# Moving four 1 MB zero fills within the order in which one Trainium2 core issues its stores

## The chip, the cores and the metric

The kernel runs on one core of a Trainium2 chip. The metric is the device time of one execution in microseconds (us); less is better. The core has a matrix engine (TensorE, PE in the profile), a vector engine (VectorE, DVE), a scalar engine (ScalarE, ACT), a general engine (GpSimd, POOL) and a synchronising engine (SyncE, SP). Data moves between device memory and on-chip memory by DMA. GpSimd and SyncE each issue DMAs on a queue of their own, and sixteen transfer engines carry out both queues.

## What is computed

The reference is one layer for a single token, forward and backward: the output and ten gradients.

```python
x = A_x
mod = (_silu(c) @ w_mod).reshape(c.shape[0], 6, 1, -1)
sa, ca, ga, sb, cb, gb = (mod[:, i].copy() for i in range(6))
h = _layernorm(x) * (1 + ca) + sa
x = x + ga * attention(h, k_cache, v_cache, wq, wo)   # last 4096 of 65536 positions
h = _layernorm(x) * (1 + cb) + sb
# FFN: D = 1024, F = 3584
g = jnp.einsum('bsd,df->bsf', h, w_gate)
u = jnp.einsum('bsd,df->bsf', h, w_up)
x = x + gb * jnp.einsum('bsf,fd->bsd', _sigmoid(g) * u, w_down)
...
_out, _vjp = jax.vjp(_f, A_x, A_k_cache, A_v_cache, A_wq, A_wo, B_w_gate, B_w_up, B_w_down, c, w_mod)
return (_out, *_vjp(grad_out))
```

Attention looks at the last 4096 of 65536 cached positions only. The gradients of the two caches have the full size, 64 MiB each, and are zero in the other 61440 positions. Writing those zeros is about half of all the bytes that the kernel moves.

## The kernel before

The zero region is cut into 120 pieces of 1 MB. The function `zero(n)` (line 153) takes the next n pieces from one list and issues each as one DMA from a tile of zeros, on GpSimd's queue (line 169). So a fill is not tied to any place in the program: the constants `Z_...` at the head of the file say how many fills stand at each point of GpSimd's instruction order, and the regions are taken in one fixed sequence. Every twelfth or thirteenth piece or so (`NARROW`) is written differently: a cursor reset, a small DMA and a DMA over 60 partitions that leaves out one of the transfer engines (lines 160 to 167).

GpSimd issues in program order. If an instruction waits, everything behind it on GpSimd waits too. Each of its DMAs uses one of eight semaphores in turn, and waits for the DMA eight places earlier to land. A fill after a matmul of the phase before the FFN also waits for that matmul ("pace").

The work is staged as follows: attention forward; the products for its weight gradients (`bch`, 64 chunks, paced by `Z_B`); folding of the modulation weights (`fold_half`, `fold_run`); then the FFN forward and backward in seven blocks of 512 hidden columns; then the remaining gradients of attention and of the modulation.

Before the FFN, `load_ug(0, ...)` issues four loads of w_up and w_gate for block 0. After them come the last chunks of `bch` with three fills (chunks 56, 58 and 60), the rest of the folding, `zero(Z_FOLD[0])`, the four loads of block 1, and `zero(Z_FOLD[1])`. `load_wd` loads the two halves of w_down on SyncE's queue.

Block 0 then runs: `front` (gate and up products), `gates` and `hh_ops` (sigmoid), `ffn_mm` (down product), `wd_ttr` (VectorE products with w_down), `wd_outer` (the gradient of w_down written over w_down by VectorE, and `store_wd` on GpSimd). This happens for two halves, and `zero(Z_FOLD[2])` follows. These are "the first w_down stores".

The loop over q then does, for each block:

- eight `ttr` on VectorE and eight `outer_act` on ScalarE, which overwrite the w_up and w_gate tiles of block q with their gradients; after the fourth, `store_ug(q, 0, 4)` and `zero(z[0])`, after the eighth, `store_ug(q, 4, 4)` and `zero(z[1])`;
- `front`, `gates`, `hh_ops` of block q + 1;
- first half of w_down of block q + 1, `load_ug(q + 2, 0, 4)`, its `store_wd`, then `zero(z[2])`;
- second half, its `store_wd`, `load_ug(q + 2, 4, 4)`, then `zero(z[3])`, and `load_wd(q + 2, ...)` on SyncE, which waits until the w_down stores have landed, since there is one w_down tile.

For the last block there is no next one, and `zero(z[2] + z[3])` follows its second `store_ug`. Here z is `Z_FFN[q]`.

Of the kernel before, what the change touches and what calls it, by code (L numbers as in the profile page):

```python
# [40 lines left out]
def spread(total, n):  # L41
    return [(i + 1) * total // n - i * total // n for i in range(n)]
# [8 lines left out]
Z_KC = [0] * 8  # L51
Z_SM = 4
Z_N = spread(31, 128)
Z_B = [n + (i in (31, 38)) for i, n in enumerate(spread(29, 43))] + [1, 1, 1, 1, 0] + [1, 1, 0, 1, 1, 0, 1, 1] + [1, 0, 1, 0, 1, 0, 0, 0]
Z_FOLD = (1, 1, 3)
Z_FFN = [(1, 1, 0, 1)] * 5 + [(1, 1, 1, 2), (1, 2, 1, 0)]
Z_END = (1, 2, 1, 0, 0)
@with_exitstack
def kernel(
# [93 lines left out]
    def zero(n, after=None):  # L153
        for _ in range(n):
            if len(zleft) <= keep[0]:
                return
            region, narrow_ = zleft.pop(0)
            first = None
            if narrow_:
                nc.gpsimd.inc_swdge_sem([], [], mode="reset_dge_cursor")  # L160
                n = nlen - ncount.pop()
                first = nc.gpsimd.dma_start(
                    out=rest[0:NS, 0:nlen * 128].rearrange("p (t x) -> p t x", t=2)[:, :, n * 64:(n + 1) * 64],
                    in_=zeros[0:NS, 0:64].rearrange("p (t x) -> p t x", t=1).broadcast_to([NS, 2, 64]))
                ins = nc.gpsimd.dma_start(
                    out=region[8:P, :].bitcast(FP32).rearrange("(t p) x -> p t x", t=2),
                    in_=zeros[0:60, :].rearrange("p (t x) -> p t x", t=1).broadcast_to([60, 2, ZW // 2]))
            else:
                ins = nc.gpsimd.dma_start(out=region.bitcast(FP32), in_=zeros[:, :])  # L169
            if after is not None:  # L170
                dep(first or ins, after)
# [437 lines left out]
    def mod_gb(ts_):  # L609
        ps = new_acc("g_ps")  # L610
        mod_tiles(ps, g_t, ts_, True, ts_[-1])
        if ts_[0] == 6:
            cp(gb, ps[:, 0:KD])
        else:
            addv(gb, gb, ps[:, 0:KD])
# [5 lines left out]
    def recent(mm, lag):  # L621
        last_mm.append(mm)
        return last_mm[-lag] if len(last_mm) >= lag else last_mm[0]
# [57 lines left out]
    def bch(n=1):  # L681
        for _ in range(n):
# [5 lines left out]
            for a in range(4):  # L688
                h = 4 * u + a
                for k in range(2):  # L690
                    mm = nc.tensor.matmul(bbank[p][k][:, :], lhsT=a4[:, p, h, :], rhs=wo_t[u][:, a, k * 512:(k + 1) * 512],  # L691
                                          start=(i == 0 and a == 0), stop=(i == 7 and a == 3))
            zero(Z_B[nbq - 1 - len(bq)], recent(mm, 3))
            if i == 7:
# [87 lines left out]
    def park(p, pl, tag):  # L782
        BT_ps[p] = pl.tile([P, D], BF16, name="BT_ps", tag=tag)
        for i in range(KD):
            nc.tensor.transpose(BT_ps[p][:, i * P:(i + 1) * P], B_t[p][:, i * P:(i + 1) * P], ident_bf[:, :])
# [64 lines left out]
    def load_wd(q, s):  # L850
        nc.sync.dma_start(out=wd_v[:, 2 * s:2 * s + 2, :], in_=wd_dram(B_w_down, q, s))
# [10 lines left out]
    def load_ug(q, j0, n):  # L862
        for k, view in ((0, wu_view), (1, wg_view)):
            nc.gpsimd.dma_start(out=ug_tile(q, k, j0, n), in_=ug_part(view, q, j0, n))
# [5 lines left out]
    def fold_half(t, k):  # L870
        ps = new_ps("fold_ps")
        for i in range(4):
            nb = 4 * k + i
            for x, src in enumerate((ga_t[t], cb_t[t], sb_t[t])):
                nc.tensor.matmul(ps[:, i * P:(i + 1) * P], lhsT=src[:, nb * P:(nb + 1) * P], rhs=ident_bf[:, :],  # L875
                                 start=(i == 0 and x == 0), stop=(x == 2), skip_group_check=True)
        nc.scalar.copy(out=w2_t[t][:, k * 512:(k + 1) * 512], in_=ps[:, :])  # L877
# [45 lines left out]
    fold_half(7, 1)  # L923
    zero(Z_FOLD[0])
    park(4, ppq, "pq")
    load_ug(1, 0, 4)
    load_ug(1, 4, 4)
    zero(Z_FOLD[1])
    mod_gb((0, 1, 2, 3, 4, 5))
# [48 lines left out]
    def wd_outer(q, s):  # L978
        for i in (2 * s, 2 * s + 1):
            outer_dve(wd_v[:, i, :], small[q % 2]["hh"][:, i:i + 1], b1k)  # L980
        store_wd(q, s)
# [30 lines left out]
    wd_outer(0, 1)  # L1012
    zero(Z_FOLD[2])
    load_wd(1, 0)
    load_wd(1, 1)
    for q in range(NB):
        z = Z_FFN[q]
        more = q + 1 < NB
# [315 lines left out]
```

## Time and profile before

| | |
|---|---|
| median of 6 runs | 600.74 us (600.02 to 601.30) |
| profiled execution | 600.27 us |
| span from its first to its last instruction | 598.5 us |
| PE / DVE / ACT / POOL busy | 68% / 55% / 48% / 28% of the span |
| moved by DMA | 246.64 MB, mean 412 GB/s |
| fills of 1 MB on GpSimd's queue | 111, median 14.6 us from issue to landing |
| gradient stores of the FFN (L868) | 28 of 512 KB, GpSimd waits 39.8 us for ScalarE before 8 of them |

Times in the profile count from the start of the span. A row of the timeline names the start, the duration, the engine, the line of the kernel, the operation, what it writes and reads, and, in brackets, how long the engine had been idle before and what ended that. A line can be that of a helper: line 169 is every full fill, line 854 every store of the gradient of w_down, line 864 every load of w_up or w_gate, line 868 every store of their gradients, line 851 every load of w_down after the first section. The share of the DMA engines can be above 1, since packets of one engine overlap.

### The profile page before, as it was taken

The page shows a single profiled execution, that of the slowest core. Times are in us where ns is not written, and L with a number is a line of the kernel's source. Part 1 is how long each engine was busy: PE and PEld are TensorE (multiplying, and loading weights), DVE is VectorE, ACT ScalarE, POOL GpSimd, SP SyncE. Part 2 cuts the span into 40 slices and gives each one's busy share as a digit, 9 for nine tenths or more (in the row PEclk, how much of TensorE's full clock was granted, in tenths as well). Part 3 has the DMA queues.
Part 4 walks back from the last instruction along what each step waited for, and adds up shares of the span by engine and source line. Part 5 has one row for each costly group of instructions (what it writes and reads, how often), then busy time and mean ns, then how long its engine had stood idle before and what let it go on. Part 6 is the DMA issues. An engine that isn't in the chain of part 4 may idle for free.

```text
span 598.5 us, 11048 instructions
## 1 busy us (share of the span) xinstructions
PE 408.3 (68%) x4587; PEld 273.7 (46%) x4612; DVE 326.9 (55%) x620; ACT 284.8 (48%) x429; POOL 166.5 (28%) x265
## 2 busy tenths in 40 slices
PE   3997688999999989999984435435444185776300
PEld 3995334334344545546664334434334155575200
DVE  3654499999511010160007495695686887878430
ACT  3489514567211014213225665865956864883200
POOL 0003123223222222222332244333343272122330
PEclk9999699999999999999995555555555586855555
DMA  8999999999999999999999999999999999999996
GB/s 349 419 418 422 412 426 417 426 424 426 428 420 427 422 426 425 425 422 423 422 402 408 418 405 409 409 411 410 410 411 416 413 408 414 421 423 426 426 415 253
DMA packets 45171, 246.64 MB, mean 412 GB/s; under 512 B 5253, under 2 KB 5253, under 8 KB 24712
## 3 DMA queue, kind: packets, MB, share of 16 engines
q0 software_dynamic: 38976, 216.55, 94.5%
q1 hardware_dynamic: 6096, 29.37, 12.5%
q8 instruction: 36, 0.59, 0.4%
q14 instruction: 15, 0.12, 0.1%
q10 hardware_dynamic: 48, 0.01, 0.0%
HBM read 60.30 MB, written 185.60 MB: 411 GB/s over the span
## 4 chain that ended last, share of the span: by engine, by line
PE 38%; DMA 32%; DVE 17%; ACT 5%; issue 5%; POOL 0%; ACTq 0%; POOLq 0%; SPq 0%; DVEq 0%
DMA out_dram<-arena 17%; PE b_ps L691 15%; PE n_ps L636 6%; DMA arena<-in_B_w_down_dram 6%; DMA out_dram<-zeros 5%; DVE arena L193 4%; DVE arena L206 3%; DVE arena L210 3%; DVE junk L210 3%; DMA arena<-in_B_w_gate_dram 3%; PE t_ps L598 2%; PE tp_wq L453 2%; PE w_ps L394 2%; PE tp_k L434 1%; ACT arena L241 1%
## 5 line engine op out<-in xcount | busy, mean ns | idle before, releaser
L169 POOL DMA_DIRECT2D out_dram<-zeros x111 | 60.8, 549 | 194.0 <-PE q_ps L471 50.7
L691 PE MATMUL b_ps<-arena 128*128 128x512 bf16 x494 | 113.4, 379 | 1.0 <-issue 0.2
L836 PE MATMUL tp_side<-ident_bf,arena 128*128 128x128 bf16 x432 | 51.7, 300 | 45.2 <-ACT arena L837 38.3
L837 ACT COPY arena<-tp_side 128x1024 bf16<-128x1024 bf16 x54 | 53.9, 1011 | 51.8 <-PE tp_side L836 51.5
L193 DVE TENSOR_TENSOR arena<-arena 128x2048 bf16<-128x2048 bf16 x64 | 76.5, 1224 | 2.3 <-PE n_ps L636 0.3
L691 PEld LDWEIGHTS <-arena 128*128 128x128 bf16 x512 | 48.7, 98 | 55.9 <-issue 2.9
L210 DVE CUSTOM_DVE_ANT_0 arena<-arena,scr 128x1024 bf16<-128x1024 bf16 x56 | 65.2, 1222 | 10.2 <-ACT scr L990 10.2
L636 PE MATMUL n_ps<-arena 128*128 128x512 bf16 x249 | 65.1, 378 | 6.9 <-DVE arena L193 5.0
L836 PEld LDWEIGHTS <-arena 128*128 128x128 bf16 x432 | 42.8, 139 | 49.6 <-issue 49.3
L241 ACT ACTIVATE arena<-scr,h 128x1024 bf16<-128x1024 bf16 x56 | 61.5, 1146 | 1.4 <-DVE dh2acc L210 1.3
L636 PEld LDWEIGHTS <-arena 128*128 128x128 bf16 x256 | 24.6, 97 | 41.6 <-issue 16.2
L210 DVE CUSTOM_DVE_ANT_0 junk<-arena,b1k 128x1024 bf16<-128x1024 bf16 x28 | 34.2, 1221 | 9.0 <-DMA arena<-in_B_w_down_dram 8.5
L868 POOL DMA_DIRECT2D out_dram<-arena x28 | 21.1, 757 | 64.3 <-ACT arena L241 39.8
L1161 ACT ACTIVATE arena<-ps_kv 128x512 bf16<-128x512 f32 x48 | 26.1, 680 | 25.8 <-PE ps_kv L1157 25.5
L202 DVE CAST arena<-b_ps 128x512 bf16<-128x512 f32 x6 | 4.2, 692 | 61.6 <-PE b_ps L691 61.6
L600 ACT CAST arena<-t_ps 128x512 bf16<-128x512 f32 x56 | 30.1, 589 | 12.1 <-PE t_ps L598 12.1
L1157 PE MATMUL ps_kv<-junk,arena 8*128 8x128 bf16 x256 | 26.5, 299 | 12.8 <-DVE arena L206 10.9
L1157 PEld LDWEIGHTS <-arena 8*128 8x128 bf16 x256 | 24.6, 138 | 14.4 <-issue 14.4
L455 ACT COPY arena<-tp_wq 128x1024 bf16<-128x1024 bf16 x23 | 21.7, 1041 | 8.2 <-PE tp_wq L453 8.2
L970 PE MATMUL fg<-hh_bf,arena 128*128 128x1 bf16 x224 | 8.2, 166 | 20.1 <-DMA arena<-in_B_w_down_dram 19.4
L877 ACT CAST arena<-fold_ps 128x512 bf16<-128x512 f32 x16 | 9.4, 587 | 24.1 <-PE fold_ps L875 24.1
L206 DVE TENSOR_SCALAR arena<-arena,cs_col 128x4096 bf16<-128x4096 bf16 (+1 forms) x16 | 16.0, 1018 | 8.6 <-DMA out_dram<-arena 8.5
(299 smaller groups left out, 644.7 us busy)
## 6 DMA issues: line engine op xcount, KB each, us to landing
out_dram<-zeros POOLq DMA_DIRECT2D x111, 1024.0 KB, 14.6
out_dram<-arena POOLq DMA_DIRECT2D x32, 1024.0 KB, 17.4
out_dram<-arena POOLq DMA_DIRECT2D x50, 512.0 KB, 9.8
out_dram<-zeros POOLq DMA_DIRECT2D x9, 960.0 KB, 14.5
arena<-in_A_wq_dram SPq DMA_DIRECT2D x8, 1024.0 KB, 20.3
arena<-in_A_wo_dram POOLq DMA_DIRECT2D x8, 1024.0 KB, 12.5
arena<-in_w_mod_dram POOLq DMA_DIRECT2D x7, 1024.0 KB, 18.6
arena<-in_B_w_down_dram SPq DMA_DIRECT2D x14, 512.0 KB, 8.8
```

Source lines behind the costliest of these rows:

```text
L169: ins = nc.gpsimd.dma_start(out=region.bitcast(FP32), in_=zeros[:, :])
L193: return nc.vector.tensor_tensor(out=out, in0=a, in1=b, op=op)
L206: return nc.vector.tensor_scalar(out=out, in0=a, scalar1=s1, scalar2=None, op0=op0)
L210: return nc.vector.tensor_tensor_reduce(out=out, in0=w, in1=b, scale=1.0, scalar=0.0, op0=ALU.mult, op1=ALU.add, accum_out=acc)
L241: return nc.scalar.activation(out=out, in_=b, func=ACT.Copy, scale=col)
L600: nc.scalar.copy(out=o, in_=ps)
L636: mm = nc.tensor.matmul(nbank[k][:, :], lhsT=k_nat[:, g, t_ * DH:(t_ + 1) * DH], rhs=vp[:, t_ % 2, 4 * k:4 * k + 4, :].rearrange("p h d -> ...
L691: mm = nc.tensor.matmul(bbank[p][k][:, :], lhsT=a4[:, p, h, :], rhs=wo_t[u][:, a, k * 512:(k + 1) * 512], start=(i == 0 and a == 0), stop= ...
L836: nc.tensor.transpose(tp[:, i * P:(i + 1) * P], blk[:, i * P:(i + 1) * P], ident_bf[:, :])
L837: nc.scalar.copy(out=blk if dst is None else dst, in_=tp[:, :])
L1157: nc.tensor.matmul(ps[:, t4 * DH:(t4 + 1) * DH], lhsT=rows[32 * g:32 * g + HG, t_ * P:(t_ + 1) * P], rhs=hd[32 * g:32 * g + HG, :], start= ...
L1161: nc.scalar.activation(out=o, in_=ps[:, :], func=ACT.Copy, scale=float(scale))
```

## The change

Three fills are taken away ahead of the first w_down stores: the one at chunk 58 of `bch` (`Z_B`), the one before the loads of block 1 and the one behind them (`Z_FOLD`). One fill is added at `zero(z[2])`, between the two w_down stores, in each of the first three passes of the loop. In the sixth pass `z[3]` goes from 2 to 3, which puts one more fill ahead of the last block's gradient stores, and in the last pass `z[2]` goes from 1 to 0, one fewer behind them. The number of fills, their regions and their sequence stay. As the narrow pieces belong to places in that sequence, one narrow piece goes from the end of the second pass's first part (behind `store_ug(1, 4, 4)`) to the end of that pass.

```diff
-Z_B = [n + (i in (31, 38)) for i, n in enumerate(spread(29, 43))] + [1, 1, 1, 1, 0] + [1, 1, 0, 1, 1, 0, 1, 1] + [1, 0, 1, 0, 1, 0, 0, 0]
-Z_FOLD = (1, 1, 3)
-Z_FFN = [(1, 1, 0, 1)] * 5 + [(1, 1, 1, 2), (1, 2, 1, 0)]
+Z_B = [n + (i in (31, 38)) for i, n in enumerate(spread(29, 43))] + [1, 1, 1, 1, 0] + [1, 1, 0, 1, 1, 0, 1, 1] + [1, 0, 0, 0, 1, 0, 0, 0]
+Z_FOLD = (0, 0, 3)
+Z_FFN = [(1, 1, 1, 1)] * 3 + [(1, 1, 0, 1)] * 2 + [(1, 1, 1, 3), (1, 2, 0, 0)]
```

## The prediction, made before the changed kernel ran

> **What bounds the kernel now.** I read first the page's slices, then the table by stretch, then GpSimd's (POOL's) timeline around the change, then the landing records of single DMAs. The slices:
>
> ```profile
> DMA  8999999999999999999999999999999999999996
> GB/s 349 419 418 422 412 426 417 426 424 426 428 420 427 422 426 425 425 422 423 422 402 408 418 405 409 409 411 410 410 411 416 413 408 414 421 423 426 426 415 253
> q0 software_dynamic: 38976, 216.55, 94.5%
> ```
>
> The transfer engines are busy from end to end; 216.55 of 246.64 MB go through GpSimd's queue. The change moves no byte, so it can act only through idle time of transfer engines. The table by stretch (us, then busy PE, PEld, DVE, ACT, POOL, clock, DMA share, GB/s) shows where the rate dips, the FFN (about 310 to 480):
>
> ```profile
> 300.00:310.00 10.00, 9.41 (x124) 6.46 (x124) 0.33 (x2) 3.29 (x6) 2.15 (x5) 1.00 1.04 395
> 320.00:330.00 10.00, 4.60 (x38) 3.94 (x38) 7.79 (x16) 6.66 (x8) 2.13 (x4) 0.50 1.08 404
> 460.00:480.00 20.00, 5.47 (x58) 3.78 (x62) 16.91 (x45) 15.12 (x16) 6.24 (x10) 0.50 1.09 411
> 560.00:580.00 20.00, 3.56 (x32) 3.29 (x31) 10.58 (x15) 2.39 (x4) 6.59 (x9) 0.50 1.01 421
> ```
>
> GpSimd's timeline (start, us, line, what, idle before and its releaser):
>
> ```profile
> 304.06 0.53 POOL L169 DMA_DIRECT2D out_dram<-zeros  x1 [3.19 <-DMA out_dram<-zeros]
> 307.58 0.53 POOL L169 DMA_DIRECT2D out_dram<-zeros  x1 [2.98 <-DMA arena<-in_w_mod_dram]
> 309.56 0.77 POOL L864 DMA_DIRECT2D arena<-in_B_w_up_dram  x1 [1.45 <-PE g_ps L344]
> ...
> 313.51 0.75 POOL L864 DMA_DIRECT2D arena<-in_B_w_gate_dram  x1 [0.86 <-DMA arena<-in_B_w_gate_dram]
> 315.73 0.56 POOL L169 DMA_DIRECT2D out_dram<-zeros  x1 [1.47 <-DMA out_dram<-zeros]
> 319.27 0.56 POOL L854 DMA_DIRECT2D out_dram<-arena  x1 [2.98 <-DVE arena L206]
> 322.70 0.53 POOL L854 DMA_DIRECT2D out_dram<-arena  x1 [2.88 <-DVE arena L206]
> 323.23 0.54 POOL L169 DMA_DIRECT2D out_dram<-zeros  x1
> ...
> 331.78 1.52 POOL L868 DMA_DIRECT2D out_dram<-arena  x2 [5.50 <-ACT arena L241]
> ```
>
> The two L854 rows are the first w_down stores. They wait for VectorE, so 319.27 and 322.70 do not depend on the fills: block 0's loads were queued ahead of them all and landed at 313. Between issues, the engines live off the backlog, which I take from the trace as bytes issued on this queue less packets ended: 3.47 MB at 319.27, 2.58 at 322.70, 2.60 at 331.78.
>
> The mean rate hides that engines differ. A DMA's semaphore rises 16 times, and the landing records give each rise. The gate load issued at 313.51 has its first rise at 319.63, ninth at 326.40, last at 328.14: the leading engine is 8.5 us ahead. From load to load the **last** rise never pauses: 2.43 us per 1 MB fill, 1.35 per up or gate load, 1.22 to 1.24 per w_down store, 1.29 per gradient store, plus about 1.25 for each w_down load on SyncE's queue. That holds at 478.55 too, where only 1.03 MB are left (1.30 per store). So the dips are leading engines running dry; the trailing ones always have work and set the end. The final DMA rises from 590.69 to 595.59; the span ends at 598.5.
>
> **The Trainium skill.** "DMA: Bandwidth & Descriptors", section "Why a DMA increments its semaphore by 16 and not by 1": up to 16 engines finish independently and only the full count means landed. The 8.5 us agree. Its section "Anatomy of one DMA — SWDGE (gpsimd) path" gives about 2.0 us fixed per DMA, mostly the receipt of the last byte, and says engines wait for no semaphore. The trace's nearest: the store of 322.70 has its first rise at 325.44, 2.74 after issue, on an engine that had idled (1.99 since its previous rise, for 1.24 of work); less 1.24 that is 1.5 fixed. I use the trace's value.
>
> **The change, part by part.**
>
> *Three fills leave the front.* One of bch 58 (304.06), Z_FOLD[0] (307.58) and Z_FOLD[1] (315.73): each one issue of 0.53 to 0.56 us on GpSimd and 2.43 on every engine. No other queue issues them. GpSimd idles there anyhow. The four loads of block 1 then go out at about 307.1 to 310.9: the first when the last fold's matmuls end (306.96), the rest as DMAs eight back land (307.30, 308.95, 310.27), since GpSimd's DMAs rotate over eight semaphores. Nobody needs them before front(1) at 334.
>
> At 319.27 the backlog is 3.47 − 3 × 1.05 = 0.32 MB, 0.8 us at 0.42 MB/us. So on average the engines run dry: at about 320.4 (the loads' slow stretch included). They restart at 319.27 plus 1.3 to 2.5 (the kernel's first fill, issued at 49.54 on an empty queue, has its first packet at 52.03), work 1.25 us, and wait for the second store, 3.43 us after the first. In mean bytes: 322.70 + (1.3 to 2.5) − 320.4 − 1.25 = 2.35 to 3.55 us lost.
>
> For the last engine: the fill of 300.31 rises last at 317.88 as before; four loads, 1.37 + 1.36 + 1.35 + 1.34 = 5.42, give 323.30; the first store 324.52 (an idle engine could show it at 319.27 + 2.74 = 322.01, so no pause); the second 325.76, against a floor of 322.70 + 2.74 = 325.44. It only just stays busy. Whether other engines start as promptly as the one behind 2.74 is not shown; the nearest row, the first SyncE load, rises over 3.84 to 4.85, 1.0 apart. So the last engine pauses 0 to 0.7; I take **0.3**. The ninth engine (321.56, then 322.80) loses 1.4, which is its lead.
>
> *Behind it.* The three Z_FOLD[2] fills follow at once (323.2 to 324.3): 7.3 us. SyncE's queue, where block 1's two w_down loads wait for these stores to land, moves from 331.91 to about 324.6 and adds 2.5: covered until 335.9. The gradient stores of 331.78 have their floor at 331.78 + 3.25 (472.58 to first rise 475.83) = 335.0 and are due at 337.2: 2.2 to spare. Those of 337.91: floor 341.2, due 335.9 + 2.58 + 2.43 + 1.29 = 342.2: 1.0 to spare, the spread between starts. I take **0.1** (0 to 0.3). In block 1 VectorE no longer waits 3.78 us for w_down; the stage runs ahead, but the engines stay the limit, so that is worth 0.
>
> *One fill per block comes in* (z[2], blocks 1 to 3), between the w_down stores: 0.55 us on GpSimd, with the second store and the next block's late loads behind it. The store comes some 3.5 us after the first, so the issue is hidden. Its 2.43 us ahead of that store delay the next w_down loads; block period then is at least (9.44 + 1.05) MB at 0.411 = 25.5 us where VectorE and ScalarE need about 22. Wait moves to w_down loads, engines stay full: 0. The narrow fill (three instructions, L160 to L165) slides from 365.3 to the end of that refill, about 10 us: 0.
>
> *The last one* goes from 481.65 to about 466. It lifts the backlog at 472.58 from 1.29 and at 478.55 from 1.03 by 1.05. The trailing engines did not pause there: 0 (in mean bytes the dip of 472 to 482 is 0.9).
>
> *Lost lead.* At 325.8 all engines stand level; before, the ninth led by 1.75. Fetches of instructions (16 KB, 15 after 325) each stop one engine for about 0.6 (64 KB takes 2.43). A lead absorbed such hits; level engines hand them to the maximum. 0 to 1.2; I take **0.3**.
>
> Sum 0.3 + 0.1 + 0.3 = 0.7: span 599.2, that execution 600.27 + 0.7 = 601.0; the median stands 0.47 above the profiled execution, so 600.74 + 0.7 = **601.4**.
>
> **Rivals.**
> *All engines starve (slower).* If the trailing engines restart as late as the mean estimate, the two stores at 319 and 322 cost 2.35 to 3.55: 603.1 to 604.3. It decides once starts on an idle queue lie over 1.5 us apart, or the trailing engines' 1.75 us were not theirs alone. For it: 0.32 MB is far below any backlog of the FFN before. Against it: the last rise goes on unpaused at 1.03 MB.
> *Lost lead is dear.* Same gap, but two or three fetches fall on engines that lost their lead: 1.2 to 2.3, so 602 to 603.
> *Filled valleys (faster).* If mean bytes count, the later valleys (0.9 at 472 to 482, some 0.4 in blocks 1 to 4) come back without the early loss: about −1.2, 599.5. Against it: those rises never paused.
> *Nothing happens.* Fills are the same bytes behind a full queue: 600.7; part of my own case.
>
> **How the numbers follow.** Little or nothing 0.50, centre 601.4 (own range 600.5 to 601.9); lost lead 0.14; all starve 0.28; faster 0.08. The range 600.1 to 604.1 leaves out the faster case and the far end of starvation. Faster and slower mean over 0.2%, 1.2 us, about what a measurement can tell: 0.08, 0.50, 0.42.
>
> **What would show it.** Block 1's loads issued by 311; the first w_down store at 319.3 landing near 324.5 (5.3 us after issue, not 12.6), the second near 326; SyncE's w_down loads at 324.6; the rate of 320 to 330 falling to some 300 to 330; that of 470 to 480 rising; the last DMA's rises closer than 4.9 us. A last rise of the second store beyond 327 means the starvation rival. I am wrong if stores at 319 shift, if the end moves without such a pause, or if the stage after 485 finds less queued than 3.7 MB.

## The result: about 1.5 us slower, and the profile after

The changed kernel takes 602.12 us in the median (601.59 to 608.10, 16 executions) against 600.62 us (600.02 to 601.89, 35 executions) for the kernel before on the same chips. The ratio is 1.0043, with a 95% interval of 1.003 to 1.0056. Ten of the 16 executions lie at 601.6 to 602.3 and six at 603.9 to 608.1; the first experiment shows what such a high one can be. The profiled execution took 601.77 us, its span 600.0 us.

The slices of the page after, the rows answering those of before:

```profile
DMA  8999999999999999999999999999999999999996
GB/s 349 420 418 421 413 425 417 426 424 425 426 425 426 421 427 424 424 423 423 419 396 340 414 405 410 414 410 411 405 410 412 425 419 412 420 427 425 423 418 270
q0 software_dynamic: 38976, 216.55, 94.3%
```

The bytes are the same. One slice, the 22nd (315 to 330 us), has fallen from 408 to 340 GB/s, a loss of 2.5 us of transfer at 408; the slice after it is down by 4 and the last slices are up. Yet the end moved by only 1.5 us. The table by stretch has the columns of the prediction's table (us, busy PE, PEld, DVE, ACT, POOL, clock, DMA share, GB/s):

```profile
300.00:310.00 10.00, 9.44 (x127) 6.45 (x126) 0.33 (x2) 3.01 (x6) 3.10 (x5) 1.00 1.04 392
320.00:330.00 10.00, 4.29 (x35) 3.64 (x35) 7.75 (x18) 6.66 (x8) 2.28 (x5) 0.50 0.90 342
460.00:480.00 20.00, 4.45 (x48) 3.58 (x46) 16.90 (x42) 14.39 (x15) 6.24 (x11) 0.50 1.12 422
560.00:580.00 20.00, 3.57 (x32) 3.30 (x31) 10.57 (x15) 2.39 (x4) 6.61 (x9) 0.50 1.01 423
```

The DMA share at 320 falls from 1.08 to 0.90: engines run dry. At 460 the rate rises from 411 to 422. The moved last fill is not what raises it here: the changed kernel without that part (e9 below) has 421 in the same stretch. GpSimd's timeline around the change:

```profile
300.04 0.56 POOL L169 DMA_DIRECT2D out_dram<-zeros  x1 [2.36 <-DMA out_dram<-zeros]
300.85 0.56 POOL L169 DMA_DIRECT2D out_dram<-zeros  x1 [0.25 <-issue]
304.69 0.77 POOL L864 DMA_DIRECT2D arena<-in_B_w_up_dram  x1 [3.28 <-PE fold_ps L875]
...
311.11 0.75 POOL L864 DMA_DIRECT2D arena<-in_B_w_gate_dram  x1 [0.81 <-PE bc_ps L297]
319.58 0.56 POOL L854 DMA_DIRECT2D out_dram<-arena  x1 [7.72 <-DVE arena L206]
323.05 0.56 POOL L854 DMA_DIRECT2D out_dram<-arena  x1 [2.92 <-DVE arena L206]
323.59 1.60 POOL L169 DMA_DIRECT2D out_dram<-zeros  x3
332.08 1.52 POOL L868 DMA_DIRECT2D out_dram<-arena  x2 [6.89 <-ACT arena L241]
```

Block 1's loads are out by 311, GpSimd then waits 7.72 us for VectorE, and the stores leave 0.3 us later than before, a drift that was there ahead of the change. What the view doesn't tell is on which transfer engine time is lost. The landing records do: sixteen rises of each DMA's semaphore, one per engine, here the first, the ninth and the last (us):

```
                                  before                      after
                            first   ninth    last      first   ninth    last
last load of block 1       319.63  326.40  328.14     316.73  321.65  323.56
first w_down store         323.45  330.13  331.85     322.31  322.93  324.88
second w_down store        325.44  331.34  333.09     325.87  325.94  326.07
first gradient store       337.09  342.36  343.80     337.12  337.28  338.72
last DMA of the kernel     590.69     -    595.59     592.88     -    597.11
```

Row 3 is the change in one line. Before, the engines stand 7.65 us apart there; after, 0.20. All leads are gone, and the last engine has lost nothing: from the last load it goes 1.32 and 1.19 on, the nominal price of one store each. Row 4 is where time lost begins to show. Three fills fewer stand ahead of it, 7.29 us, and this execution was 0.31 behind already at the loads of block 0; so from the 343.80 of before the last rise was due at 336.82, and it came at 338.72, 1.9 later. The fifteenth rise is at 337.49 and the sixteenth at 338.72, so one engine has fallen 1.2 us behind all others, and that one now is the end of the queue.

To compare ends, I count the megabytes that each GpSimd DMA adds to its queue and read the last rise at equal counts (interpolated between DMAs; in brackets the spread from first to last rise). Kernels not yet named are the experiments below; all are profiled executions:

```
MB issued            100      115            140            180            200            216.5
before            292.83   333.22 (7.6)   402.25 (4.7)   506.01 (2.3)   556.50 (4.6)   595.51 (4.9)
after             293.21   335.40 (1.7)   403.75 (2.1)   508.94 (3.2)   558.04 (4.0)   597.04 (4.2)
e9  no last part  293.03   335.26 (1.7)   403.69 (2.3)   508.83 (3.3)   557.93 (4.2)   596.93 (4.4)
e4  two fills     293.15   333.57 (2.5)   402.35 (3.7)   507.53 (2.6)   557.72 (4.6)   596.73 (4.8)
e10 one fill      292.95   333.45 (5.2)   402.15 (5.0)   506.08 (2.2)   556.79 (4.7)   595.80 (4.9)
e7  two ahead     293.36   333.69 (3.6)   402.48 (4.3)   506.64 (4.4)   555.94 (5.3)   594.68 (5.3)
e11 more lead     292.90   333.41 (9.9)   404.03 (3.4)   508.18 (3.6)   557.63 (4.9)   597.35 (5.9)
```

After against before: +0.38 at 100 MB (drift of this execution, ahead of everything changed), +2.18 at 115 MB, +1.5 at 140, +2.9 at 180, +1.53 at the end. The 115 MB of after and e9 can't be read against the others: SyncE's loads of w_down go out 7 us earlier there, and at that point 23.46 MB of SyncE's queue have moved in place of 22.55. Those 0.91 MB are worth about 2.2 us at the 1.25 us of a load, so they make up the whole difference. In the other columns the rows have equal bytes of SyncE's queue behind them, to 0.04 MB. The loss of the front is therefore the 1.9 us seen at the first gradient stores, and later stretches give and take about 1 us at a time.

### The profile page after: what moved, and what is told of

Its sections match the earlier page's. It is cut to its first block, busy times and chain, and to the rows that moved or that the text cites. A ratio compares the mean times of both kernels' runs of the same rounds, so it can differ in the third digit from the quotient of the medians.

```text
span 600.0 us, 11044 instructions
## 1 busy us (share of the span) xinstructions
PE 409.5 (68%) x4587; PEld 276.6 (46%) x4612; DVE 326.7 (54%) x620; ACT 285.2 (48%) x429; POOL 167.5 (28%) x265
## 4 chain that ended last, share of the span: by engine, by line
DMA 35%; PE 34%; DVE 16%; ACT 8%; issue 4%; POOL 0%; ACTq 0%; POOLq 0%; SPq 0%; DVEq 0%
DMA out_dram<-arena 16%; PE b_ps L691 11%; DMA out_dram<-zeros 9%; DMA arena<-in_B_w_gate_dram 6%; PE n_ps L636 6%; DVE arena L193 4%; DVE arena L206 4%; ACT arena L241 3%; DMA arena<-in_B_w_down_dram 3%; DVE junk L210 3%; DVE arena L210 2%; PE t_ps L598 2%; PE tp_wq L453 2%; PE w_ps L394 2%; PE tp_side L836 1%
## 5 line engine op out<-in xcount | busy, mean ns | idle before, releaser
L691 PEld LDWEIGHTS <-arena 128*128 128x128 bf16 x512 | 48.8, 98 | 55.8 <-issue 2.9
L210 DVE CUSTOM_DVE_ANT_0 arena<-arena,scr 128x1024 bf16<-128x1024 bf16 x56 | 65.2, 1220 | 10.3 <-ACT scr L990 10.3
L836 PEld LDWEIGHTS <-arena 128*128 128x128 bf16 x432 | 44.1, 141 | 54.0 <-issue 53.7
L636 PEld LDWEIGHTS <-arena 128*128 128x128 bf16 x256 | 24.6, 97 | 41.6 <-issue 16.2
L953 PE MATMUL fg<-h_bf,arena 128*128 128x1 bf16 x448 | 14.6, 166 | 14.6 <-DMA arena<-in_B_w_gate_dram 9.7
L953 PEld LDWEIGHTS <-arena 128*128 128x128 bf16 x448 | 14.0, 105 | 15.4 <-DMA arena<-in_B_w_gate_dram 10.2
```

The source lines that it names most:

```text
L210: return nc.vector.tensor_tensor_reduce(out=out, in0=w, in1=b, scale=1.0, scalar=0.0, op0=ALU.mult, op1=ALU.add, accum_out=acc)
L636: mm = nc.tensor.matmul(nbank[k][:, :], lhsT=k_nat[:, g, t_ * DH:(t_ + 1) * DH], rhs=vp[:, t_ % 2, 4 * k:4 * k + 4, :].rearrange("p h d -> ...
L836: nc.tensor.transpose(tp[:, i * P:(i + 1) * P], blk[:, i * P:(i + 1) * P], ident_bf[:, :])
L953: nc.tensor.matmul(gu[:, col + i:col + i + 1], lhsT=ug_v[:, q % 2, j // 4, j % 4, k, f0:f0 + 255:2], rhs=h2_bf[:, j:j + 1], start=(j == 0) ...
```

## The experiments

**The front alone.** Three fills leave the front and go behind the first two w_down stores; nothing goes into the blocks.

```diff
-Z_B = [n + (i in (31, 38)) for i, n in enumerate(spread(29, 43))] + [1, 1, 1, 1, 0] + [1, 1, 0, 1, 1, 0, 1, 1] + [1, 0, 1, 0, 1, 0, 0, 0]
-Z_FOLD = (1, 1, 3)
+Z_B = [n + (i in (31, 38)) for i, n in enumerate(spread(29, 43))] + [1, 1, 1, 1, 0] + [1, 1, 0, 1, 1, 0, 1, 1] + [1, 0, 0, 0, 1, 0, 0, 0]
+Z_FOLD = (0, 0, 6)
```

> The three fills leave the front as in the change, but go straight behind the first two w_down stores (six fills there in place of three); the loop and the last block are as before. Lost lead (my theory): the backlog at the first w_down store falls to 0.3 MB, the sixteen engines stand level after the second store (rises within 0.3 us), and the time rises as with the whole change, by 1 to 3 us. Loop placement (rival: the fills between the w_down stores in blocks 1 to 3 cost): 0 to +0.3 us. Full pause (rival: all engines stop for 2.35 to 3.55 us): last rise of the second store at 327 or later, +2.4 to +3.6 us.

Measured 602.55 us (602.07 to 606.79, 18 executions) against 600.67, ratio 1.0047 (1.003 to 1.0063). So the front alone makes the whole loss. Ten executions lie at 602.1 to 602.6, eight at 604.2 to 606.8. The profiled one is a high one, 606.79 us. GpSimd's timeline there, at the first two w_down stores:

```profile
324.15 0.56 POOL L854 DMA_DIRECT2D out_dram<-arena  x1 [10.74 <-issue]
327.62 0.56 POOL L854 DMA_DIRECT2D out_dram<-arena  x1 [2.92 <-DVE arena L206]
```

The first leaves 4.9 us later than the 319.27 of the kernel before; for its wait of 10.74 us the view names no releaser ("issue"). TensorE's timeline of the same execution shows why:

```profile
310.77 0.61 PE L785 MATMUL BT_ps<-ident_bf,scr 128*128 128x128 bf16 x8
311.21 1.14 PE L344 MATMUL g_ps<-cs_bf,arena 128*128 128x1 bf16 x40
315.48 0.35 PE L344 MATMUL g_ps<-cs_bf,arena 128*128 128x1 bf16 x8 [3.12 <-DMA arena<-in_w_mod_dram]
```

TensorE ends the last fold at 310.77, in the kernel before at 306.96. It then waits 3.12 us for a piece of w_mod, whose load SyncE had issued 3.8 us late too (299.20 against 295.39). The sixteen rises of the first store lie at 326.89 to 327.07: every engine had been idle, the last one too. Of the second they lie at 331.16 to 332.25. The kernel before has its 3.47 MB (8 us) queued against such a delay, the changed one 0.54 MB (0.32 had been worked out). I had not thought of that.

The delay is older than the missing fills. The table by stretch for 250 to 260 us, in the kernel before, here, and in the kernel with two fills ahead at the back (e7 below, front as before):

```profile
250.00:260.00 10.00, 8.42 (x101) 4.91 (x101) 4.08 (x10) 1.17 (x2) 2.20 (x4) 1.00 1.13 423
250.00:260.00 10.00, 8.47 (x93) 4.74 (x92) 2.74 (x8) 1.17 (x2) 2.19 (x4) 0.77 1.13 422
250.00:260.00 10.00, 8.47 (x93) 4.76 (x92) 2.74 (x8) 1.17 (x2) 2.23 (x5) 0.76 1.13 420
```

In the second and third the granted clock is 0.5 for 6.83 us from 255 us on, and the run of `b_ps` matmuls there takes 13.0 us in place of 10.3. Both end the last fold 3.8 us late, at 310.77 and 310.73. The first w_down store of e7 leaves 4.5 us late:

```profile
323.72 0.56 POOL L854 DMA_DIRECT2D out_dram<-arena  x1 [6.96 <-DVE arena L206]
```

But 1.90 MB are still queued there, where the front alone has nothing left, and that execution took 599.43 us, the median of its kernel being 599.40. The same lateness of TensorE costs nothing with the three fills in front, and 4.6 us (606.79 against the usual 602.2) without them.

**A late TensorE made on purpose.** Twenty matmuls are put in front of `fold_half(4, 0)`, 0.22 us each and 4.5 in all; nobody reads their result. Once in the kernel before, once in the changed one.

```diff
+    late_ps = new_ps("late_ps")
+    for _ in range(20):
+        nc.tensor.matmul(late_ps[:, :], lhsT=ident_bf[:, :], rhs=wo_t[7][:, 0, 0:512], start=True, stop=True)
     fold_half(4, 0)
```

> The kernel before with 20 more matmuls of 128x512 on TensorE in the fold stage (their result is read by nobody), so that everything TensorE feeds, the first w_down stores too, comes about 4.3 us later. Cover (my theory of the slower executions): the backlog of 3.5 MB, 8 us, hides it, so within 0.6 us of before. If the delay itself costs, whatever is queued: +2 to +4 us.

> The same 20 matmuls in the changed kernel. Cover: with 0.3 MB queued nothing hides the delay; all engines stop, the last rise of the second w_down store goes from 326 to about 330, and the time is 3.5 to 4.5 us over the changed kernel's usual 602.1, so 605.5 to 606.5. If the late stores are covered by something else: within 1 us of the changed kernel.

Before, with the delay: 602.18 us (600.81 to 607.53, 22 executions) against 600.72. Eleven of the 22 stand at 600.8 to 601.6, half a microsecond over the kernel before, as expected; the other eleven at 602.8 to 607.5. The profiled one is of the latter. Its TensorE timeline, at the last piece of w_mod:

```profile
322.89 0.37 PE L344 MATMUL g_ps<-cs_bf,arena 128*128 128x1 bf16 x8 [6.29 <-DMA arena<-in_w_mod_dram]
```

And its GpSimd timeline, the last fill and the first w_down store:

```profile
317.65 0.56 POOL L169 DMA_DIRECT2D out_dram<-zeros  x1
332.04 0.56 POOL L854 DMA_DIRECT2D out_dram<-arena  x1 [13.82 <-issue]
```

TensorE ended the last fold at 315.01, 8.05 us late: the 4.5 of the matmuls, and 3.5 of a stretch of half clock as above (0.76 between 250 and 260 us). Then it waited 6.29 us for w_mod. The store left 12.8 us late; the last fill had landed at 330.74, the store at 334.98. Even 3.47 MB are used up then. The mean granted clock agrees for the highest: 0.765 to 0.767 in the six executions above 606.8, 0.768 to 0.771 in the eleven low ones. It does not set the five between apart (0.768 to 0.774). The changed kernel with the delay: 607.30 us (606.25 to 608.48, 4 executions), 5.2 over the changed kernel. Its table by stretch against that of the changed kernel's 342 and 418:

```profile
320.00:330.00 10.00, 5.52 (x71) 4.99 (x72) 7.62 (x18) 4.08 (x5) 2.70 (x5) 0.50 0.41 136
330.00:340.00 10.00, 3.92 (x54) 3.43 (x51) 8.67 (x17) 9.54 (x10) 2.06 (x3) 0.50 1.12 425
```

So 4.5 us of delay cost half a microsecond with the three fills in front (in the lower half of the executions) and 5.2 without (in four executions). The expectation of at most 0.6 for the kernel before held only for that half.

**The loop alone.** Three fills are taken from the very end (`Z_END`) and put at z[2] of the first three blocks, where the change has them. Front and last block are as before.

```diff
-Z_FFN = [(1, 1, 0, 1)] * 5 + [(1, 1, 1, 2), (1, 2, 1, 0)]
-Z_END = (1, 2, 1, 0, 0)
+Z_FFN = [(1, 1, 1, 1)] * 3 + [(1, 1, 0, 1)] * 2 + [(1, 1, 1, 2), (1, 2, 1, 0)]
+Z_END = (1, 0, 0, 0, 0)
```

> The front is as before; one more fill stands between the w_down stores of blocks 1, 2 and 3, taken from the end of the kernel (Z_END gives up its second and third place). Lost lead: no gap at 319, so within 0.6 us of before. Loop placement: the blocks get longer and the time rises by 1 to 3 us.

600.86 us (599.89 to 606.60, 14 executions) against 600.67, ratio 1.000 (0.998 to 1.0021). Where the fills go costs nothing clear of noise; that they leave the front does.

**The last part alone.**

```diff
-Z_FFN = [(1, 1, 0, 1)] * 5 + [(1, 1, 1, 2), (1, 2, 1, 0)]
+Z_FFN = [(1, 1, 0, 1)] * 5 + [(1, 1, 1, 3), (1, 2, 0, 0)]
```

> Only the fourth fill moves, from behind the last block to ahead of its gradient stores. Trailing engines set the end: no change, within 0.5 us. Mean bytes set the end: the dip at 472 to 482 (0.9 us of transfer in mean bytes) goes and the time falls by 0.5 to 0.9 us.

599.47 us (598.83 to 601.08, 22 executions) against 600.67, ratio 0.9979 (0.997 to 0.9988): faster by 1.2. I had put 0 there. The table by stretch, where the kernel before has a DMA share of 1.09 and 411 GB/s:

```profile
460.00:480.00 20.00, 5.47 (x58) 3.85 (x62) 16.91 (x46) 15.09 (x16) 6.68 (x11) 0.50 1.12 422
```

The leading engines, which ran dry there before, now have work. At 486 to 498 us the rises of a DMA lie 3.96 us apart, in the kernel before 2.13: they keep their lead.

**Fewer and more fills.** Two (chunk 58 and the one before block 1's loads, z[2] = 1 in two blocks, last part as before), one (chunk 58, z[2] = 1 in one block, last part as before), and five (the change, and chunks 56 and 60 too, z[2] = 1 in five blocks). The edits of `Z_B` follow from the chunks named; the rest, in that order:

```diff
-Z_FOLD = (1, 1, 3)
-Z_FFN = [(1, 1, 0, 1)] * 5 + [(1, 1, 1, 2), (1, 2, 1, 0)]
+Z_FOLD = (0, 1, 3)
+Z_FFN = [(1, 1, 1, 1)] * 2 + [(1, 1, 0, 1)] * 3 + [(1, 1, 1, 2), (1, 2, 1, 0)]
```

```diff
-Z_FFN = [(1, 1, 0, 1)] * 5 + [(1, 1, 1, 2), (1, 2, 1, 0)]
+Z_FFN = [(1, 1, 1, 1)] * 1 + [(1, 1, 0, 1)] * 4 + [(1, 1, 1, 2), (1, 2, 1, 0)]
```

```diff
-Z_FOLD = (1, 1, 3)
-Z_FFN = [(1, 1, 0, 1)] * 5 + [(1, 1, 1, 2), (1, 2, 1, 0)]
+Z_FOLD = (0, 0, 3)
+Z_FFN = [(1, 1, 1, 1)] * 5 + [(1, 1, 1, 3), (1, 2, 0, 0)]
```

> Only two of the three front fills move (chunk 58 and the one before block 1's loads), one each into blocks 1 and 2; the last block as before. Backlog at the first store about 1.4 MB. Lost lead: engines in the middle lose part of their 1.75 us, the rises of the second store spread over 1.5 to 2 us, time +0.2 to +1.0 us. Full pause or a cost per fill in the loop: two thirds of the whole change, +1 to +2 us.

> The changed kernel with the two remaining fills ahead of the first w_down stores (chunks 56 and 60) moved as well, into z[2] of the next two blocks. Lost lead with the trailing engine just busy at three: each further fill is a whole pause, so 602.1 + 2 x 2.43 = about 607. If the engines had already stopped at three, the same slope. If something else fills the gap: 602 to 603.

> One fill only (chunk 58) leaves the front and goes into the first block's middle; the rest as before. About 2.4 MB stay queued when the first w_down store is issued. Lost lead: the lead of the ninth engine over the last shrinks at the second store's landing but does not vanish, so 0.2 to 0.7 over before: two fills cost 1.1. If what counts is only whether all engines run dry, this costs 0: same as before within 0.2.

One: 600.69 us (600.01 to 606.61, 22 executions) against 600.79, ratio 1.0008 (0.9996 to 1.002), no difference clear of noise; 2.31 MB are queued at the first store. Four of the 22 lie at 603.5 to 606.6, though, and none of the 43 of the kernel before beside them is above 602.2. Two: 601.74 (600.94 to 604.58, 22 executions) against 600.67, ratio 1.002 (1.001 to 1.0031); 1.34 MB queued. Five: 607.43 (606.36 to 608.18, 4 executions), ratio 1.0104; nothing is queued, and the first store's rises lie at 323.20 to 323.39. The table by stretch with five:

```profile
310.00:320.00 10.00, 7.17 (x175) 6.58 (x173) 4.70 (x13) 2.85 (x7) 2.23 (x3) 0.80 0.69 240
320.00:330.00 10.00, 4.63 (x50) 3.92 (x49) 7.76 (x16) 6.44 (x7) 2.70 (x5) 0.50 0.71 257
```

From three to five fills the time grows by 5.3, that is 2.65 per fill, the 2.43 of its transfer and a little: past three, every byte taken away is a pause of all sixteen. (The five rest on four executions, and the profiled one, 608.01, had the half clock at 255 us too. The lowest of each lie 4.8 apart, 2.4 per fill.) From none to three the time grows by 0, 1.1 and 1.5. With two, the last engine does not pause either; in the table of ends it stands with the kernel before up to 140 MB (402.35, less than the 0.3 of drift over it) and is 1.5 over at 180. Its loss falls in block 4 (counted from 0). The table by stretch there, before and with two, and the first w_down store of that block with two:

```profile
420.00:430.00 10.00, 3.92 (x37) 3.40 (x35) 9.12 (x17) 9.09 (x10) 3.83 (x6) 0.50 1.05 407
420.00:430.00 10.00, 4.07 (x32) 3.42 (x33) 8.60 (x20) 7.55 (x9) 2.64 (x4) 0.50 1.02 359
418.33 0.56 POOL L854 DMA_DIRECT2D out_dram<-arena  x1 [1.90 <-DMA arena<-in_B_w_down_dram]
```

The second store left at 421.77 there, before at 418.73, and a fetch of instructions fell at 431.4. The cost of fills taken from the front need not fall at the front. Whether the smaller lead (2.71 us between the rises of the second store) makes that valley, or the shifted timetable of the loop, no run separates. In the late execution of e7 the same rises were 3.60 apart, and it lost nothing.

**The change without its last part.**

```diff
-Z_FFN = [(1, 1, 1, 1)] * 3 + [(1, 1, 0, 1)] * 2 + [(1, 1, 1, 3), (1, 2, 0, 0)]
+Z_FFN = [(1, 1, 1, 1)] * 3 + [(1, 1, 0, 1)] * 2 + [(1, 1, 1, 2), (1, 2, 1, 0)]
```

> The changed kernel without its last part: the sixth pass keeps (1, 1, 1, 2) and the last (1, 2, 1, 0); the three fills still leave the front and go into the first three blocks. If the two parts add, this stands at the changed kernel's 602.1 plus the 1.2 that the last part gained on its own, so about 603.3, 2.6 over before, and the last DMA's rises lie no closer than after's 4.2 us. If the last part gains nothing once the transfer engines have been levelled at the FFN's start, it stands at 602.1. Below 601.5 neither holds.

601.99 us (601.57 to 605.83, 13 executions) against 600.79, ratio 1.0027 (1.0014 to 1.0041). That is the changed kernel's time. The two parts don't add: the last part gains 1.2 behind the old front and nothing behind the new one.

**More lead, and a better end.** First the front turned round, with the last part of the change; then the old front with two fills ahead of the last block's gradient stores.

```diff
-Z_FOLD = (1, 1, 3)
-Z_FFN = [(1, 1, 0, 1)] * 5 + [(1, 1, 1, 2), (1, 2, 1, 0)]
+Z_FOLD = (2, 2, 1)
+Z_FFN = [(1, 1, 0, 1)] * 5 + [(1, 1, 1, 3), (1, 2, 0, 0)]
```

```diff
-Z_FFN = [(1, 1, 0, 1)] * 5 + [(1, 1, 1, 2), (1, 2, 1, 0)]
-Z_END = (1, 2, 1, 0, 0)
+Z_FFN = [(1, 1, 0, 1)] * 5 + [(1, 1, 1, 4), (1, 2, 0, 0)]
+Z_END = (0, 2, 1, 0, 0)
```

> The change turned round at the front: the fill before the loads of block 1 and the one behind them become two each, both taken from the three behind the first w_down stores; and the last fill is moved ahead as in the kernel that moved it alone, 599.5. About 5.5 MB stay queued at the first w_down store. If a lead is worth time, the spread of the second store's rises grows beyond the 7.8 us of that kernel and the end comes earlier, by up to 1 us: 598.5 to 599.3. If 3.5 MB already give all the lead that is used, it stays at 599.5. If the stores are held up by GpSimd's wait for the DMA eight places back, the first store leaves later than 319.5 and the gain is lost: 599.5 to 600.5.

> The kernel before, with two fills (not one) moved from behind the last block's gradient stores to ahead of them. Lost lead: the leading engines do not run dry at 472 to 482, the rises at 486 spread over 4 us or more in place of 2.1, and the time falls as with one fill or slightly more, 599.0 to 599.6. Mean bytes: no further dip to fill, so the same as with one fill. If the gain with one fill was chance: 600.2 to 600.9.

More lead: 601.32 us (600.23 to 603.36, 14 executions) against 600.79, so 1.7 to 1.9 over the last part alone (against its own kernel before, and directly). At the first store 3.68 MB were queued, not 5.5. Two things went against it. GpSimd held the first store up, as its timeline has it:

```profile
323.47 0.53 POOL L854 DMA_DIRECT2D out_dram<-arena  x1 [2.22 <-DMA out_dram<-zeros]
```

The releaser is no longer VectorE but a fill landing, the DMA eight places back, which the third guess had foreseen, with too small a price. And the two fills that moved forward are missing one block later. The table by stretch there:

```profile
350.00:360.00 10.00, 4.08 (x35) 3.33 (x33) 8.56 (x20) 6.82 (x7) 2.79 (x5) 0.50 0.92 330
```

The same stretch of the kernel before:

```profile
350.00:360.00 10.00, 3.66 (x31) 3.17 (x31) 9.33 (x17) 8.90 (x10) 3.92 (x6) 0.50 1.05 403
```

The leads are gone at 360 (spread 1.87 at the load issued at 353.63, from 9.9 at 333) and the next DMA of that queue has its last rise 1.9 behind the fifteenth. It is the changed kernel's history, one block later. Two ahead: 599.40 us (598.93 to 600.54, 21 executions) against 600.72, ratio 0.9977 (0.997 to 0.9984). That beats both kernels by 0.2% and 0.5%, and is no better than the last part alone.

## Why the prediction was right and where it was wrong

The time, 602.1, lies inside the range of 600.1 to 604.1, 0.7 above the 601.4 named. It is not in the range of the likeliest case (600.5 to 601.9) but in that of the rival "Lost lead is dear" (602 to 603), which had 0.14. Slower by over 0.2% came out, where 0.42 stood against 0.50 for no difference. The sum gave 0.7 and the medians differ by 1.5: the width of the range, drawn for a rival that did not come true, did part of the work.

*The last engine's pause at the second store, 0.3 (0 to 0.7).* It was 0. The first store landed 5.3 us after its issue, as said; the second's last rise is 326.07, where 325.76 was worked out and 0.31 of drift comes on top. The choice of the last rise in place of mean bytes was right: the mean would have 2.35 to 3.55 lost, and the rates per microsecond of 319 to 326 do lose 2.6 us against 425 GB/s, but on engines that had a lead. That answers the rival "All engines starve" for the ordinary execution. It is true with two more fills gone (five) or 4.5 us of delay, at 2.65 per fill and 5.2.

*Later gradient stores, 0.1.* Those of 332.08 had their fifteenth rise at 337.49, due at 337.2. The 1.2 of the sixteenth is a hit on one engine, so it belongs to the next term.

*Lost lead, 0.3 (0 to 1.2).* This is the term of the sum that was mis-sized. It measured about 1.1 at the end (1.53 less 0.38 of drift), and 1.9 at the first gradient stores. Two things fit the difference. A fetch of instructions was taken as 0.6 us, scaled from larger packets; the records have 36 fetches of 16 KB at 0.88 to 1.14 us, median 1.02, and the last rise jumps by as much where one falls on the last engine: in the changed kernel from 488.64 to 491.04 for a store of 1.29, with a fetch at 488.7; in the kernel with the last part alone from 510.57 to 514.11 for a fill of 2.43, with a fetch at 511.3. And the w_down loads on SyncE's queue, due on all engines at once after the levelling, did not fall on them evenly: from the second store to the first gradient store the first rise was 0.18 over its nominal sum, the ninth 0.27, the last 1.57. A fetch of 0.94 us started at 334.6 in the same stretch, so uneven loads and a fetch are not told apart there. That a fetch is what stops an engine is read from the times; the trace doesn't name the engine. Nor did an experiment hold the w_down loads back: with the fills gone they go out at 324.94 in place of 331.91, onto level engines, and what is due to the earlier loads and what to the lost lead stays open. The Trainium skill, "Runtime: NRT & Kernel Launch", section "Instruction fetch mechanics", says that a sequencer refills in blocks of 16 KiB and that the cost is "mostly hidden". No run here measured the engine that executes; for a transfer queue that sets the end, the two jumps above are 1.11 us each over the nominal price.

*z[2] in the blocks, 0.* Right: 600.86 against 600.67 with that alone.

*The last one moved, 0.* Wrong on its own: 1.2 gained. The argument was that trailing engines did not pause there. They did not, but a leading engine that runs dry loses a lead, the same thing that I priced at the front and left out at the back. Between 180 and 200 MB the kernel before needs 50.49 us, the kernel with two ahead 49.30, the changed one 49.10 after having been 2.9 late. The changed kernel without its last part needs 49.10 there as well, so the moved fill is not what catches up behind the new front. How a kept lead becomes 1.2 with the old front, and why not behind the new one, isn't settled: it may depend on which engine is at the back when the next hit comes, and the records don't show which engine is which. That both versions with the old front whose spread is 4 or more at 180 MB (4.05 with the last part alone, 4.37 with two ahead) gain it, over 22 and 21 executions, speaks against chance in single executions.

*What was to show it.* SyncE's w_down loads went out at 324.94, said was 324.6. The rate of 320 to 330 us was 342 GB/s, a little above the 300 to 330 named. That of 460 to 480 rose, though not for the reason given (421 without the moved fill). The last DMA's rises lie 4.24 us apart, closer than the 4.89 of before.

*What was not in the sum.* The cover against a late TensorE. The prediction treated the stores at 319 as fixed and named only "if stores at 319 shift" as a way to fail. In the first experiment's profile they did shift, by 4.9 us, after a stretch of half clock some 50 us ahead of the first missing fill. Six of the 16 executions of the changed kernel lie above 603.9; of the 149 of the kernel before that stood beside the experiments, four. That these six have the same cause is inferred: their mean granted clock is 0.761 to 0.767, that of the other ten 0.765 to 0.772, and none of the six was profiled.

## What to carry to other kernels

In a kernel bound by its DMA queue, ask for the rises of single engines, and not only for the mean rate: bytes queued at a wait are worth nothing to the mean as long as the last engine has work, but they hold the leads that can take the next hits, and they cover a late producer. Take a fill from such a place only down to the point where leads survive (here the median with 2.3 MB left queued was unchanged, though 4 of 22 executions ran high; 1.3 MB cost 1.1 us, 0.5 MB cost 1.5 us and 5.2 more once TensorE came 4.5 us late). When executions of one kernel differ by several microseconds, compare the granted clock ahead of the change, too. Look for places where the leads do run dry and move work there: one constant, 1.2 us.

## What the runs showed of the hardware

- Sixteen engines that had stood 7.65 us apart were level to 0.20 us after one near-empty queue (the second w_down store, 325.87 to 326.07), and kept within 1.6 to 4.3 us of each other from the first gradient stores to the end, 270 us on. At 140 MB, near 403 us, the rises lay 2.1 apart, in the kernel before 4.7.
- An engine that had nothing to do starts evenly: on empty queues the sixteen rises of a 512 KB store came 2.73 to 2.94 us after its issue, 0.15 to 0.19 apart (the front alone, both delayed kernels, and the one with five fills). The 1.0 to 1.5 us between starts that the prediction allowed for was not seen.
- Fetches of 16 KB of instructions take 1.02 us of one transfer engine in the median, where packets of 8 KB of data have 0.35 us (in the changed kernel's records).
- The granted clock of TensorE is not the same in every execution of these kernels at the same place: four of the thirteen profiled ones (the front alone, the delayed kernel before, two ahead, five fills) have 0.5 for 6.83 us from 255 us on, the other nine have 1.0 there.
